# RWKV-6 attention and an MLP on one core: the first round wholly on TensorE, one layout for k and r, integer additions on GpSimd

## The chip, the cores and the metric

The kernel runs on one core of a Trainium2 chip. The metric is the device time of one execution in microseconds (us), the median over several executions. Engines are named as in the profile: PE is TensorE, DVE is VectorE, ACT is ScalarE, POOL is GpSimd, and SP issues most DMAs.

## The reference

Two blocks follow each other; the inputs are fp32 except the two MLP weights, which come as float64, and the output is fp32. The first is a recurrence over 768 steps for 4 batches of 8 heads, each with a 48 x 48 state; w is a decay of each row of the state and lies between 0.8 and 0.95.

```python
batch, n_heads, seq, head_dim = (4, 8, 768, 48)
for t in range(S):
    kt, vt, rt, wt = (k[:, :, t], v[:, :, t], r[:, :, t], w[:, :, t])
    cur = np.einsum('bhd,bhe->bhde', u[None] * kt, vt)
    y[:, :, t] = np.einsum('bhd,bhde->bhe', rt, state + cur)
    state = wt[:, :, :, None] * state + np.einsum('bhd,bhe->bhde', kt, vt)
```

The second takes y as x of shape (4, 768, 384): a layer norm without offset, a product to 1536 columns, a relu, a product back to 384, and x added.

```python
xn = (x - mu) / np.sqrt(var + 1e-06) * g_ln
ch = np.maximum(xn @ w_ch1, 0.0) @ w_ch2
return (x + ch).astype(np.float32)
```

## The kernel before

**Rounds and tiles.** The work is cut into 8 rounds (a batch and half of its 768 steps), each of 3 tiles of 128 steps. Round 0 alone is worked in two parts: tile 0, and then tiles 1 and 2 (`parts_of_round`). A round has a front (the recurrence) and a back (layer norm and MLP). The MLP of round 0 uses fp32 weights as they come; rounds 1 to 7 use weights split into halves and differences, the last four rounds for both products.

**The recurrence in chunks.** Steps are taken in chunks of 64 (`C`). Within a chunk, a matrix A holds for each pair of steps (s, t) the weight with which v of step s enters y of step t. It is built by levels: at level n, blocks of 2^n steps are joined in pairs. k of the left block is multiplied by the decay from its step to the block's end, r of the right block by the decay from the block's start to its step; the products k x r of such pairs are one batch of small PE products (`quads`, into a PSUM tile named `a`), and `keep` (a masked copy, DVE) or `keep_last` (ACT) puts them into A. `grow` then multiplies k and r by the totals of w over the block (`totals`), so that the next level can join blocks twice as long. There are 6 levels (0 to 5).

**Levels 0 and 1 and the diagonal.** Before the change these are not done by PE. `inner` multiplies on tiles in natural layout (steps on partitions, four steps of a group beside each other, `Q = 4`): it writes k and r with the first two levels' decays into padded tiles `pad_k` and `pad_r` (48 values of a head in 64 places), the 4 x 4 terms of each group of four steps into `vals`, and the total decay of four steps into `w4`. `inner_by_tile` sends `vals` through DRAM (`own_d`, four DMAs out and three back into `va`), so that it lies by partition, and `place` writes it into A with a mask. `turn` has PE transpose the padded tiles into `kr` (head dimension on partitions, two heads in rows 0 to 47 and 64 to 111), `turn_w` does it for `w4`. `quads` and `grow` then start at level 2 (`LOW`). This holds for every round; in round 0 `grow` works on k and r apart and, in its second part, on half of the heads apart (two to four instructions a level); in rounds 1 to 7 `grow_both` does k and r in one instruction, which the layout of `kr` allows there.

**The rest of the front.** `turn_k` turns k back, `states` makes the chunks' states on PE and scans them on DVE, `exchange_r` and `swap` copy r and states to the other half of the partitions, and `outputs` makes y and x.

**Weights.** The 24 pieces of w_ch1 and w_ch2 are given as float64 and taken apart by `convert`: ACT makes the upper bits (`upper`), the lower bits (`lower`) and the sign; DVE shifts the upper word by 3 (`shift`) and adds the two as integers (`join`), each on 384 columns.

**What sets the order.** Every instruction is registered by `plan.add` with a list of engines that it could run on, a cost, and what it reads and writes. The order and the choice of engine are not found when the kernel is built: `ORDER` is a list of numbers in the class `Plan`, one for each registered step in the order of issue (10000 or 20000 added names the second or third engine of its list). Each engine works its instructions in that order. While it goes through the list, `order` estimates times from the costs, and where PE would wait for more than 0.35 us it issues `idle` products of zeros into a free PSUM bank instead; their number comes from that estimate and is fixed in the built program. A GpSimd step that shares the SBUF port with DVE gets a dependency on the DVE steps before it, by the flag `port`. All instructions are issued through one helper, `InOrder.call`, so the profile gives L46 as the line of nearly all of them: they are told apart by their tiles.

Of the kernel before, what the change touches and what calls it, by code (L numbers as in the profile page):

```python
# [62 lines left out]
class Plan:  # L63
# [11 lines left out]
        4, 3, 11, 7, 9, 8, 2, 12, 14, 13, 272, 5, 271, 0, 268, 269, 15, 267, 18, 19, 20, 10021, 10016, 6, 10023,  # L75
        270, 24, 25, 26, 275, 22, 111, 274, 273, 17, 29, 276, 277, 30, 280, 282, 281, 278, 105, 10279, 38, 113,
        27, 28, 114, 39, 36, 37, 123, 106, 112, 107, 124, 286, 115, 283, 284, 285, 10, 289, 125, 31, 290, 71,
        40, 291, 126, 293, 108, 99, 32, 10297, 10033, 1, 10034, 45, 294, 288, 287, 46, 47, 49, 109, 43, 127,
        129, 484, 51, 42, 41, 100, 103, 117, 131, 132, 130, 292, 295, 118, 296, 101, 44, 50, 10035, 10298, 48,
        52, 110, 53, 54, 55, 57, 128, 56, 310, 60, 102, 304, 301, 303, 481, 58, 133, 121, 64, 61, 63, 62, 66,  # L80
        302, 147, 72, 311, 65, 77, 119, 59, 67, 68, 120, 135, 313, 312, 315, 104, 10299, 149, 78, 79, 150, 116,
        134, 73, 307, 305, 122, 486, 148, 69, 80, 74, 137, 136, 436, 75, 138, 70, 76, 306, 308, 314, 309, 183,
        141, 153, 317, 318, 319, 323, 151, 487, 485, 483, 351, 482, 488, 316, 489, 81, 139, 152, 84, 140, 185,
        82, 83, 438, 85, 86, 320, 154, 10186, 87, 321, 88, 201, 322, 324, 325, 143, 451, 89, 326, 90, 327, 91,
        328, 329, 155, 184, 144, 156, 142, 331, 332, 333, 341, 330, 334, 145, 335, 342, 343, 338, 344, 187, 491,
        336, 146, 300, 340, 10092, 95, 345, 97, 353, 93, 352, 492, 10495, 354, 10494, 337, 339, 346, 347, 357,
        350, 349, 96, 94, 358, 98, 259, 348, 203, 355, 356, 361, 493, 453, 490, 497, 496, 360, 359, 455, 364,
        257, 506, 213, 362, 260, 215, 202, 216, 363, 499, 507, 247, 258, 10500, 10502, 165, 245, 255, 159, 214,
        160, 248, 177, 10365, 10366, 368, 243, 246, 367, 369, 370, 371, 372, 374, 161, 10373, 244, 256, 249,
        250, 377, 378, 379, 380, 375, 251, 376, 501, 10162, 508, 498, 503, 20204, 10517, 178, 509, 252, 510,  # L90
        179, 189, 669, 672, 171, 505, 504, 10180, 217, 205, 181, 163, 157, 188, 383, 384, 675, 524, 521, 514,
        207, 182, 439, 158, 164, 516, 511, 673, 522, 523, 670, 674, 421, 515, 190, 512, 397, 387, 513, 385, 166,
        425, 398, 218, 671, 530, 173, 386, 191, 192, 452, 525, 677, 167, 195, 456, 208, 168, 531, 518, 381, 393,
        466, 172, 169, 170, 423, 174, 175, 193, 533, 395, 176, 426, 534, 454, 194, 526, 527, 422, 437, 676, 388,
        382, 389, 390, 394, 261, 10679, 10519, 10678, 529, 265, 266, 253, 399, 254, 196, 262, 457, 263, 403,
        400, 528, 532, 206, 396, 197, 460, 424, 680, 211, 199, 463, 681, 264, 209, 536, 537, 10683, 391, 198,
        219, 237, 238, 410, 404, 468, 220, 210, 442, 392, 440, 538, 535, 539, 200, 685, 543, 684, 212, 540, 223,
        441, 231, 225, 555, 556, 401, 233, 221, 232, 415, 411, 544, 402, 239, 682, 222, 545, 235, 416, 234, 551,
        470, 427, 546, 227, 224, 547, 557, 687, 542, 552, 686, 241, 10688, 548, 228, 240, 430, 553, 445, 550,
        226, 10428, 10520, 10443, 10446, 10689, 691, 693, 558, 429, 863, 692, 549, 461, 462, 559, 560, 433, 412,  # L100
        554, 541, 405, 694, 406, 467, 236, 229, 242, 230, 561, 565, 10690, 562, 413, 471, 431, 469, 458, 414,
        566, 567, 563, 564, 695, 472, 478, 568, 464, 10434, 696, 10569, 10570, 448, 698, 697, 407, 711, 710,
        864, 860, 865, 709, 857, 702, 10449, 10705, 10706, 571, 572, 573, 574, 575, 576, 703, 444, 475, 577,
        10580, 579, 578, 704, 408, 447, 862, 712, 459, 435, 432, 450, 465, 581, 589, 590, 582, 473, 409, 591,
        583, 592, 713, 861, 417, 585, 699, 418, 608, 474, 603, 593, 715, 623, 858, 714, 479, 859, 480, 476, 700,
        701, 586, 718, 707, 584, 866, 587, 588, 419, 716, 609, 594, 719, 604, 610, 595, 624, 596, 628, 477, 618,
        10867, 10869, 721, 625, 605, 597, 626, 629, 611, 717, 720, 722, 868, 873, 630, 612, 724, 725, 874, 723,
        619, 631, 620, 632, 627, 870, 606, 10875, 613, 633, 598, 638, 634, 614, 621, 635, 607, 879, 708, 876,
        871, 796, 743, 643, 599, 727, 615, 616, 600, 617, 636, 622, 728, 637, 741, 739, 872, 644, 10877, 601,
        645, 733, 1048, 602, 880, 726, 730, 734, 735, 646, 736, 745, 731, 738, 10878, 881, 884, 737, 886, 742,  # L110
        647, 653, 639, 746, 648, 420, 826, 1050, 781, 744, 1051, 1045, 729, 885, 732, 786, 1052, 897, 654, 890,
        747, 748, 740, 892, 640, 891, 753, 749, 887, 641, 655, 754, 888, 10755, 750, 751, 889, 882, 883, 900,
        816, 1046, 658, 649, 1049, 1047, 1055, 893, 10894, 10895, 642, 1057, 659, 1053, 898, 1056, 752, 756,
        757, 650, 906, 899, 901, 651, 663, 660, 1054, 1061, 1059, 11062, 931, 11060, 11058, 11063, 11064, 11066,
        904, 10758, 759, 761, 760, 762, 763, 764, 765, 1067, 652, 10767, 10768, 10766, 777, 778, 779, 656, 664,
        773, 661, 1069, 11065, 657, 1068, 907, 769, 770, 771, 774, 775, 1138, 903, 1087, 1141, 902, 811, 665,
        801, 1135, 1136, 780, 776, 662, 772, 905, 1072, 896, 909, 911, 910, 1074, 787, 788, 1073, 802, 666, 797,
        908, 667, 912, 913, 1143, 817, 914, 1140, 932, 791, 818, 789, 819, 803, 790, 804, 792, 820, 805, 915,
        1075, 821, 831, 1086, 1088, 1142, 1137, 1139, 916, 1085, 1004, 836, 1144, 793, 1076, 798, 794, 1070,
        795, 1071, 1077, 799, 800, 782, 822, 924, 783, 823, 926, 925, 784, 921, 824, 927, 919, 785, 922, 920,  # L120
        923, 806, 832, 1078, 984, 1497, 1089, 1090, 1091, 918, 928, 917, 11081, 1079, 825, 833, 1080, 937, 933,
        807, 812, 934, 11145, 11146, 11147, 1092, 938, 834, 929, 808, 813, 814, 809, 846, 1148, 815, 810, 11149,
# [215 lines left out]
def kernel(  # L338
# [116 lines left out]
    for i in range(FC):  # L455
        plan.hold("h", f"held{i}")
        tile_("h", f"held{i}", [P, RN])
# [1315 lines left out]
    def front(part):  # L1773
# [29 lines left out]
        for lev in range(LOW, NLEV):  # L1803
            for us in apart:
                quads(part, lev, us)
# [96 lines left out]
```

## Time and profile before

| | us |
|---|---|
| median of 3 executions | 502.27 (501.8, 502.27, 507.67) |
| the profiled execution | 506.6 |
| its span, first to last instruction | 504.9 |
| DVE busy in the first 50 us | 41.9 |
| ACT busy in the first 50 us | 35.1 |
| DVE busy from 60 to 110 us | 48.5 |

The page of the profile gives busy time for each engine, then the span in 40 slices of 12.6 us, in which each digit is a busy share in tenths, the DMA traffic, the chain of work that ended last, and the costliest groups of instructions. A group's line has the engine, the operation, the tile that it writes, what it reads, the shape, and a count; then busy time and the mean duration of one in ns; then the idle time of that engine just before, and what ended it. Products in fp32 show two passes on PE for each instruction, transposes one. Where PE has an instruction named `idle`, its time is filler. Two rows of the page that the steps below rest on are these, the grow steps of all rounds together and the chain:

```profile
PE 75%; DVE 9%; ACT 9%; issue 2%; DMA 2%; SPq 1%; DVEq 0%; ACTq 0%
L46 DVE TENSOR_TENSOR kr<-kr,tot 112x1536 f32<-112x1536 f32 (+1 forms) x52 | 59.5, 1154 | 18.2 <-PE a L46 17.5
```

Grouped by shape, these 52 are 28 whole ones of 1536 columns (1787 ns each) and 24 of round 0 with 256 columns (415 ns each).

### The profile page before, as it was taken

Reading aid. Unit: us, or ns where it says so; the run is one execution under the profiler, and the core shown is the slowest. Engines: PE = TensorE matmul, PEld = TensorE weight load, DVE = VectorE, ACT = ScalarE, POOL = GpSimd, SP = SyncE. Lnnn points to the kernel's source line nnn. Section 1 sums busy time; section 2 is a strip of 40 time slices with the busy share of each in tenths; the row PEclk is TensorE's granted clock in tenths of the full one; section 3 lists DMA queues with packets and bytes.
Section 4 is the critical chain, followed back from the end, with each engine's and each line's share of the span. In section 5 each row is a group of like instructions: output and inputs, shape, how many; then the busy total and the mean of one; then the engine's idle time right before and its main releaser. Section 6 shows DMA issues by size and latency. Waiting matters only on the chain.

```text
span 504.9 us, 17798 instructions
## 1 busy us (share of the span) xinstructions
PE 488.0 (97%) x7718; PEld 408.5 (81%) x7718; DVE 359.8 (71%) x733; ACT 261.0 (52%) x596; POOL 101.3 (20%) x106
## 2 busy tenths in 40 slices
PE   9999998999999899999999899989999999999995
PEld 5676887567877578876798676778999999999995
DVE  6997899998856882696975597888957354454434
ACT  2897977954474227525545435459732333342230
POOL 6301405440224600613430530000130000000000
PEclk9998999999999999999999799999999999999999
DMA  7787374559683374237476603251231212314301
GB/s 206 185 237 210 101 193 140 106 138 231 179 233 65 65 185 114 22 97 193 81 195 165 143 4 62 23 128 28 63 111 48 62 48 78 95 48 126 95 0 47
DMA packets 105758, 57.43 MB, mean 114 GB/s; under 512 B 61904, under 2 KB 102352, under 8 KB 105680
## 3 DMA queue, kind: packets, MB, share of 16 engines
q1 hardware_dynamic: 105408, 56.10, 43.1%
q8 instruction: 60, 0.98, 0.8%
q10 hardware_dynamic: 272, 0.20, 0.1%
q14 instruction: 18, 0.15, 0.1%
HBM read 45.86 MB, written 8.06 MB: 107 GB/s over the span
## 4 chain that ended last, share of the span: by engine, by line
PE 75%; DVE 9%; ACT 9%; issue 2%; DMA 2%; SPq 1%; DVEq 0%; ACTq 0%
PE h_ps L46 27%; PE a L46 22%; PE o L46 15%; PE o_2P L46 3%; PE kr_ps L46 2%; DVE A L46 2%; PE idle L46 2%; PE o_2D L46 2%; PE xT_ps L46 2%; DVE kr L46 1%; ACT rest L46 1%; SPq L46 1%; PE kn_ps L46 1%; ACT rx L46 1%; ACT A L46 1%
## 5 line engine op out<-in xcount | busy, mean ns | idle before, releaser
L46 PE MATMUL o<-ffn,h 128*128 128x384 f32 x288 | 103.7, 501 | 0.1
L46 PEld LDWEIGHTS o<-ffn,h 128*128 128x128 f32 x288 | 53.1, 193 | 29.9 <-issue 1.2
L46 DVE TENSOR_TENSOR kr<-kr,tot 112x1536 f32<-112x1536 f32 (+1 forms) x52 | 59.5, 1154 | 18.2 <-PE a L46 17.5
L46 ACT ACTIVATE h_ps<-h_ps 128x384 f32<-128x384 f32 x84 | 39.3, 475 | 63.2 <-PE h_ps L46 58.1
L46 DVE SCALAR_TENSOR_TENSOR hL<-h_ps,hH 128x384 fp32r<-128x384 f32 x48 | 26.5, 555 | 56.8 <-ACT hH L46 56.7
L46 PEld LDWEIGHTS a<-kr 48*56 48x56 f32 (+3 forms) x3072 | 40.9, 123 | 13.3 <-issue 6.5
L46 PE MATMUL h_ps<-xd,d 128*128 128x384 f32 x204 | 50.8, 355 | 0.4 <-DMA d<-w1d 0.4
L46 PE MATMUL a<-kr 48*56 48x32 f32 (+3 forms) x3072 | 45.8, 209 | 5.0 <-issue 3.2
L46 ACT ACTIVATE hH<-h_ps 128x384 fp32r<-128x384 f32 x48 | 23.6, 491 | 48.9 <-PE h_ps L46 48.9
L46 PE MATMUL h_ps<-xhl,wl 128*128 128x384 f32 x180 | 43.8, 351 | 0.0
L46 PE MATMUL h_ps<-xhl,wh 128*128 128x384 f32 x180 | 41.2, 337 | 0.0
L46 PEld LDWEIGHTS h_ps<-xd,d 128*128 128x128 f32 x204 | 36.5, 190 | 3.1 <-PE h_ps L46 0.7
L46 ACT COPY kr<-kr_ps 112x512 f32<-112x512 f32 x48 | 27.0, 586 | 20.3 <-PE kr_ps L46 20.1
L46 PE MATMUL idle<-nought 128*128 128x384 f32 (+1 forms) x114 | 35.7, 442 | 1.3 <-DVE eps L46 1.0
L46 ACT ACTIVATE h<-h_ps 128x384 f32<-128x384 f32 (+2 forms) x60 | 24.7, 426 | 21.5 <-PE h_ps L46 21.5
L46 PEld LDWEIGHTS h_ps<-xhl,wl 128*128 128x128 f32 x180 | 31.1, 188 | 1.7 <-ACT h_ps L46 0.3
L46 PE MATMUL a<-xkr,hH 128*128 128x384 f32 x96 | 32.4, 337 | 0.0
L46 PEld LDWEIGHTS h_ps<-xhl,wh 128*128 128x128 f32 x180 | 32.3, 188 | 0.0
L46 PEld LDWEIGHTS idle<-nought 128*128 128x128 f32 x114 | 21.2, 203 | 11.8 <-issue 2.3
L46 DVE SCALAR_TENSOR_TENSOR hD<-hH,hL 128x384 fp32r<-128x384 f32 x48 | 26.7, 565 | 0.8
L46 PE MATMUL h_ps<-xf,w 128*128 128x128 f32 (+1 forms) x144 | 26.1, 333 | 0.0
L46 PE MATMUL a<-vx,A 64*64 64x48 f32 x384 | 24.8, 222 | 1.2 <-issue 1.2
(171 smaller groups left out, 1102.8 us busy)
## 6 DMA issues: line engine op xcount, KB each, us to landing
d<-w1d SPq DMA_DIRECT2D x84, 192.0 KB, 3.0
raw<-in_moe_w_ch_dram SPq DMA_DIRECT2D x24, 384.0 KB, 4.2
nat_r<-in_r_dram SPq DMA_DIRECT2D x24, 192.0 KB, 3.7
nat_w<-in_w_dram SPq DMA_DIRECT2D x24, 192.0 KB, 3.6
v<-in_v_dram SPq DMA_DIRECT2D x24, 192.0 KB, 4.6
nat_k<-in_k_dram SPq DMA_DIRECT2D x23, 192.0 KB, 3.8
w1d<-w1diff SPq DMA_DIRECT2D x12, 192.0 KB, 2.9
out_dram<-x SPq DMA_DIRECT2D x4, 576.0 KB, 4.0
```

Of the source, the lines that this page charges most:

```text
L46: ins = self.tc.keep_in_program_order(f(*args, **kw))
```

## The change

Round 0 and the weights are touched; rounds 1 to 7 keep their computation.

1. Round 0 makes all six levels on PE. `inner`, `turn_w` and `inner_by_tile` are not called for it. `turn` takes k and r from the natural tiles, and `whole_row` does the same for w: for each step of a group, `by_head` transposes one head and the 16 columns behind it to rows 0 to 63 and multiplies the second head by the identity to rows 64 to 111. The whole w lies in a third tile of the kind of `kr`, named `low0`, which also takes the totals of level 1. `lowest` is 0 for round 0, so that `quads`, `grow`, `keep` and `totals` run for levels 0 and 1 too, with two more masks.
2. The diagonal of A in round 0 is made by `own_terms`: r is multiplied by u (`ru`), one batch of 64-column products follows, and a masked copy with the mask `diagonal` takes it into A, which is set to zero at the start. u is loaded twice, by head dimension (`u_t`).
3. `kr` lies as [2, tile, pair of heads, step] instead of [2, unit, pair and tile, step], in all rounds, so that one `grow` handles k and r for either part.
4. The 24 integer additions of `convert` (`join`) run on GpSimd. The 12 shifts of w_ch1 are done in 4 instructions of 1152 columns; what waits for the addition is kept in tiles of the home `wl` instead of `h`.
5. In round 0 some copies out of PSUM, and in all rounds the halves `upper` and `scale`, may be given to DVE by the order (`shared`, `copy_on`); costs and port flags in `plan.add` are changed in some places, which issues nothing by itself. `ORDER` is replaced as a whole (2014 steps instead of 2062).

```diff
+    def by_head(to, name, c, s, rows):
+        row = tiles[name][:, c].rearrange("p j s d -> p (j s d)")
+        PE.transpose(to[0:HP], row[rows, ds(s * D, HP)], ident[rows, rows])
+        PE.matmul(to[ds(HP, D)], tiles[name][rows, c, 1, s], ident[rows, rows], start=True, stop=True)
...
+                        if rnd == 0:
+                            by_head(to[:, n, s], f"nat_{nm}0", c, s, rows)
+                            continue
                         PE.transpose(
...
+    def lowest(part):
+        return LOW if part[0] else 0
...
+    def whole_row(part):
...
+                t = tile_("a", ps, None)[0:PD, :, 0 : Q * C].rearrange("p i (a k s) -> p i s k a", a=NA, s=Q)
+                for s in range(Q):
+                    for i in range(2):
+                        by_head(t[:, i, s], "nat_w0", c, s, ds(C * i, C))
...
+    def own_terms(part):
...
+            BY[e].tensor_tensor(out=to, in0=R, in1=u_, op=ALU.mult)
...
+                            PE.matmul(
+                                t[ds(C * (i ^ j), C), j, a, c],
+                                K[rows, c0 + c, a, ds(C * i, C)], R[rows, c, a, i],
+                                start=True, stop=True,
+                            )
...
+            DVE.copy_predicated(
+                out=to, data=ps.rearrange("s b (c t) -> s b c t", c=nc),
+                mask=diagonal[:, None, None].broadcast_to([P, 2 * NA, nc, C]),
+            )
...
-    def grow(part, lev, nm, us=both_units):
...
-    def grow_both(part, lev):
+    def grow(part, lev):
         rnd, c0, nc = part
+        n, half, mine = 1 << lev, U * W, nc * NA * P
...
+            X = X[:, n : n + 2 * (half - n)].rearrange("p (m z) -> p m z", m=2)
+            X = X[:, :, ds(c0 * NA * P, mine - n)].rearrange("p m (q n) -> p m q n", n=n)[:, :, 0::2]
...
         def join():
             bits = value_().bitcast(I32)
-            DVE.tensor_tensor(out=bits, in0=bits, in1=tiles[rest_].bitcast(I32), op=ALU.add)
+            POOL.tensor_tensor(out=bits, in0=bits, in1=rest(), op=ALU.add)
...
-        plan.add("DVE", 0.353, shift, w=[key], pri=first, port=True)
-        plan.add("DVE", 0.552, join, r=[rest_], w=[key], pri=first, port=True)
+        if not first:
+            plan.add("DVE", 0.353, shift, w=[key], pri=soon, port=True)
+            plan.add("POOL", 1.05, join, r=[rest_], w=[key], pri=soon)
+        elif i % KC == KC - 1:
+            keys = [(key[0], kc) for kc in range(KC)]
+            plan.add("DVE", 0.769, shift, w=keys, pri=soon, port=True)
+            for kc in range(KC):
+                plan.add("POOL", 1.05, late[i - KC + 1 + kc], r=[(rest_[0], kc)], w=[keys[kc]], pri=soon)
...
-        inner(part)
-        turn_w(part)
+        if rnd:
+            inner(part)
+            turn_w(part)
+        else:
+            whole_row(part)
...
-        inner_by_tile(part)
-        apart = [[uu] for uu in both_units] if rnd == 0 and nc > 1 else [both_units]
-        for lev in range(LOW, NLEV):
...
+        if rnd:
+            inner_by_tile(part)
+        else:
+            own_terms(part)
+        for lev in range(lowest(part), NLEV):
+            quads(part, lev)
+            grow(part, lev)
```

## The prediction

> **What bounds the kernel now.** I read four views. First the page's busy shares and slices: TensorE has work in 488.0 of the 504.9 us, so its stream decides, provided that it is useful work.
>
> ```profile
> PE 488.0 (97%) x7718; PEld 408.5 (81%) x7718; DVE 359.8 (71%) x733; ACT 261.0 (52%) x596; POOL 101.3 (20%) x106
> PEclk9998999999999999999999799999999999999999
> L46 PE MATMUL idle<-nought 128*128 128x384 f32 (+1 forms) x114 | 35.7, 442 | 1.3 <-DVE eps L46 1.0
> ```
>
> It is not all useful: 114 passes (57 instructions) multiply zeros. Second, the timeline of TensorE for the first 60 us shows where they stand.
>
> ```profile
> 0.98 10.69 PE L46 MATMUL idle<-nought 128*128 128x384 f32 x28 [0.98 <-DVE eps L46]
> 11.60 0.44 PE L46 MATMUL kr_ps<-ident,pad_r 64*112 64x64 f32 x8
> ...
> 12.95 2.98 PE L46 MATMUL idle<-nought 128*128 128x384 f32 x10
> ...
> 24.93 0.49 PE L46 MATMUL idle<-nought 128*128 128x128 f32 x2
> 25.35 0.64 PE L46 MATMUL a<-kr 48*60 48x32 f32 x32
> 25.93 0.45 PE L46 MATMUL kn_ps<-ident,kr 48*128 48x48 f32 x8
> ...
> 27.70 1.14 PE L46 MATMUL idle<-nought 128*128 128x384 f32 x4
> ```
>
> The reader is to see that the first turn of k and r starts at 11.60, although k and r landed by 4.54 (the first VectorE multiplication of them starts then): VectorE has to make the padded tiles first. From each filler group's start to the next work the 26 groups take 34.3 us, 32 of them before 52 us. After about 52 us TensorE streams real work. Third, the table of busy time by ten microseconds and finer has the granted clock; two stretches stand out.
>
> ```profile
> 42.00:43.00 1.00, 1.00 (x6) 0.67 (x3) 1.00 (x3) 0.83 (x4) 0.00 (x0) 0.57 1.04 359
> 283.00:285.00 2.00, 2.00 (x5) 1.13 (x4) 1.97 (x3) 0.70 (x2) 0.84 (x1) 0.50 0.35 71
> ```
>
> The clock is near 0.5 from 42 to 45.5 and from 281 to 287.5, some 10 us of half speed, worth about 5 us. Fourth, the waits: after 55 us TensorE waits little (the scaled x 1.8 us, the matrix A 1.6, x 0.7, and "issue" 4.7 over the whole span).
>
> The profiled execution took 506.6 us (span 504.9 and 1.7 around it), 4.3 above the median of 502.27; one of the two slow stretches would explain that much. My sum is a difference made on the profiled execution, carried over to the median.
>
> **Part by part: the fillers (removed).** The number of fillers is in the program. Before: 26 groups, 34.3 us. After: 30 groups, smaller: 15 of one 128-column instruction, 5 of 256, 6 of 384+128, 1 of 384+256, 3 of 384+384+128, one of which opens the program. Prices from start to next start: 128 columns 0.42 (24.93 to 25.35); 384+128 1.07 (27.70 to 28.77); 384+384+128 1.61 (29.44 to 31.05). For 256 and 384+256 I estimate 0.6 and 1.3 between those. The opening group meets the slow start (its first passes stand 0.64 apart until 4.34, then 0.32): 3.0. Sum 15x0.42 + 5x0.6 + 6x1.07 + 1.3 + 2x1.61 + 3.0 = 23.2. Saved: 11.1. Two groups of before were stretched (1.92 in the slow clock, 1.53 late), so 9.7 is the low end.
>
> **TensorE work (added).** Levels 0 and 1 of the products are new in round 0: 96 instructions, six blocks of 16. A block lasts 25.93-25.35 = 0.58: 3.5 us. The own terms are 48 instructions with 64 columns instead of 32, three blocks; TensorE's 16-instruction v blocks with 64 partitions last about 0.5, so I take 0.6 each: 1.8. The turn of a tile goes from 16 single-pass transposes (0.6 us, 18.17 to 18.80) to 16 of them and 16 true products of two passes, 48 passes. The quad blocks put 32 passes into 0.58 when four parts of the array run together, so 48 take 0.87: +0.25 for each of 3 tiles, 0.75. The w turn is 24 passes a tile, 0.45, three times, against 0.4 now: +0.95. Sum 7.0. Bounds: 5 if the small tiles pack like the v blocks, 10 if the products of half tiles do not run beside the transposes. I take 7.0, as nearly all of it is priced by rows of the same kind.
>
> **VectorE in round 0 (moved).** Gone: about 25 multiplications and sums on natural tiles (13.4 us by their rows), four placings of A (2.2), 24 halves of grow (24x0.415 = 10.0). New: twelve whole grows (0.145+0.00105 per column fits the rows 0.41 at 256 and 1.76 at 1536, so six at 0.68 and six at 1.22: 11.4), six extra masked copies (4.1 at 0.43 and 0.69 for the halves and up to 1.23 for the whole diagonal), r by u 1.9, products of w 2.3, copies out of PSUM about 4. Up to the last state scan of round 0 (before: 49.2 us) its list by these prices, less the 0.08 by which successive rows overlap, is some 33 us from 5.3, so it does not forbid an earlier end; the chain over the levels (product, copy, grow) is what the fillers stand for, and they are in the sum already.
>
> ScalarE has 17 instructions fewer, and it is half idle.
>
> **Queues (SP, GpSimd).** Fourteen small DMAs of round 0's way through DRAM go off SP's queue, with their 2.5 to 4.5 us to landing. Two loads of u with 4-byte rows come in, the second as SP's fifth. SP issues one each 0.6 us, so it goes out at about 3.5 and lands near 7.1 (g_sb and u_bc: 3.8 and 3.6 us). VectorE's second copy-out is at about 6.5, and behind it stands r by u, then everything of VectorE. That is 0.6 us. On GpSimd five masks instead of three are built at the start; a mask takes 1.6 to 2.0 us there (3.78 to 5.42, 5.48 to 7.5). Level 0's is first and in time, level 1's last, at about 12.3; VectorE's masked copy of level 1 is due near 11.6 and all of VectorE stands behind it: 0.7. I add both and 0.2 for the r tile of part 1, since fillers are laid for gaps and not for these: +1.5 (0 to 3).
>
> **Integer additions to GpSimd (moved).** 24 additions leave VectorE (0.547 and 0.550 each, 13.2 us), 24 shifts become 16 (1 us less). VectorE gets about 8 us back, because multiplications of later rounds move to it from GpSimd. GpSimd's price for an int32 addition of 384 columns is not in the trace; its float rows of that shape:
>
> ```profile
> L46 POOL TENSOR_TENSOR w1diff<-wh,wl 128x384 fp32r<-128x384 f32 x5 | 5.2, 1042 | 3.6 <-ACT wl L46 3.5
> L46 POOL TENSOR_TENSOR w2t<-ffn,xkr 128x384 f32<-128x384 f32 x2 | 2.7, 1355 | 11.6 <-ACT xkr L46 11.6
> ```
>
> So 25 to 33 us on an engine that is 20% busy, and idle from 28 to 44 us. After 55 us TensorE is the bound, and what VectorE gains there can only shorten the 4.1 us of waits named above: I take -1.0, between -4.1 and a loss (rival two).
>
> **Sum.** -11.1 + 7.0 + 1.5 - 1.0 = -3.6. On the profiled execution 503.0; beside the median 502.27, 498.7: I say 498.5.
>
> **Rivals.** *One, more is won (faster).* The new order also removes the other 3.1 us of waits after 55 us, the 1.6 us "issue" stop at 279.4, and the early half-speed stretch (1.7): -3.6-3.1-1.6-1.7 = -10, 492; if the median's executions hold the late half-speed stretch too, which follows that stop within a microsecond, 3.3 more, 489. For it: each of these is a place where the order decides, and the early stretch lies in round 0. Against: the late fillers are 7 units of 128 columns before and 8 after, so the program itself still expects such gaps.
>
> *Two, the GpSimd additions hold up VectorE (slower).* The trace shows the mechanism at one place: a placing of A (two inputs in SBUF) lasts 3.39 us beside a GpSimd multiplication from 161.63 to 164.78.
>
> ```profile
> 161.63 3.15 POOL L46 TENSOR_TENSOR nat_k<-nat_k,u_bc 128x1152 f32<-128x1152 f32 x1
> 162.21 3.39 DVE L46 TENSOR_TENSOR A<-va,mask_and 128x768 int32<-128x768 int32 x1
> ```
>
> At 0.69 for 512 columns it would be 1.0 alone; it ended 0.8 us after GpSimd did. If each addition holds a grow for its whole length (1.2), the twelve of w1 put 14 us into the opening, and half of the others 7 more where VectorE is 97% busy (60 to 110 us): -3.6+21 = +17, 520. The point: 0.15 us per addition (3.6/24) eats the gain, 0.6 (13.6/24) makes a loss over 2%. Against: from 95.67 to 105.48 GpSimd multiplications last 1.43 to 1.62, near their shortest, beside a VectorE that is over 90% busy; the additions can lie beside VectorE's reads of PSUM, of which there are now more. The Trainium skill, SBUF — State Buffer, "Who interferes with whom", speaks against this part of the change: a VectorE instruction with two SBUF inputs and a GpSimd one that reads SBUF exclude each other for a whole instruction. This trace agrees at the row above (3.39 against 1.0); by that rule alone, with nothing lying well, the time would be the 520.
>
> *Three, the opening is eaten up (no gain).* Fillers keep the clock up. Now 40 units at the start become 7, ending near 4.0, before the passes speed up at 4.34. If a stretch or two of half speed like that of 42 to 45.5 (1.7 us lost) falls into the early products, or the half-tile turns don't overlap (+3), the time is 501 to 506. The Trainium skill, TensorE: Matmul & The Clock Gate, Part 1, has the clock low by default and up only after some 3.4 us of activity in a free-running window; the trace agrees in the 0.64 and 0.32 spacing, though its clock column shows 1.00 there. Taken alone, that rule would add one such stretch, 500.
>
> **Numbers.** Forecast 0.40 (494 to 501), rival one 0.37 (485 to 492), rival three 0.12 (501 to 506), rival two 0.11 (512 and up). Within 2% is 492.2 to 512.3, about what a measurement of this kernel can tell from no change: 0.40+0.12 = 0.52; faster 0.37; slower 0.11. The range 485 to 508 takes in the bounds of the TensorE work (-2, +3) and of the queues (-1.5, +1.5) and leaves out rival two.
>
> **What would show it.** In the profile after: fillers near 23 us with the first kr_ps before 5 us (else the fillers' step is wrong); a<-kr of two new forms 48*63 and 48*62 and a<-ru together near 5.3 us; TensorE without fillers from about 46 us instead of 52; GpSimd additions at 1.0 to 1.4 with grow rows still at 0.68, 1.22 and 1.79. Grow rows stretched by a microsecond beside additions mean rival two; granted clock near 0.5 before 30 us means rival three; no gap at all between 55 and 340 us means rival one.

## The result and the profile after

The changed kernel took 553.04 us (median of 4 executions, 552.54 to 561.73) beside 502.03 for the kernel before on the same chip: a ratio of 1.0987 (1.0904 to 1.107), 10% slower, outside the range of 485 to 508. The ratio is of means and leaves out the execution of 561.73, which ran slow as a whole. Its profiled execution took 553.54, span 551.8: 46.9 us more than the span of before.

The page of the changed kernel, busy shares, slices of VectorE and of the clock, and the fillers:

```profile
span 551.8 us, 18599 instructions
PE 533.9 (97%) x8143; PEld 439.4 (80%) x8143; DVE 361.0 (65%) x707; ACT 256.0 (46%) x579; POOL 109.9 (20%) x120
DVE  3113566867888968937878669979876644634434
PEclk7555767997999999999999999999999999999999
L46 PE MATMUL idle<-nought 128*128 128x128 f32 (+2 forms) x86 | 33.1, 506 | 1.0 <-DVE eps L46 1.0
```

TensorE is 97% busy as before, so the share alone tells nothing. Taking the fillers off its busy time does: 488.0 - 35.7 = 452.3 before, 533.9 - 33.1 = 500.8 now. TensorE's own work grew by 48.5 us; fillers fell by 2.6, and time without any work grew by 1.0. The sum is the 46.9 of the spans. The slices say where: the clock is 0.5 to 0.7 in the first seven, and VectorE is 10 to 30% busy in the first four. The timeline of TensorE there (start, duration, count of passes):

```profile
4.25 3.37 PE L46 MATMUL kr_ps<-ident,nat_r 64*64 64x64 f32 x24
7.55 4.98 PE L46 MATMUL kr_ps<-ident,nat_k 64*64 64x64 f32 x24
12.46 4.98 PE L46 MATMUL a<-ident,nat_w 64*64 64x64 f32 x24
...
18.09 1.08 PE L46 MATMUL a<-kr 48*63 48x32 f32 x32
...
21.32 4.98 PE L46 MATMUL kr_ps<-ident,nat_r 64*64 64x64 f32 x24
26.22 4.98 PE L46 MATMUL kr_ps<-ident,nat_k 64*64 64x64 f32 x24
```

Nine such rows of 24 passes, one each for r, k and w of three tiles, stand in the first 55 us. The first row takes 3.30 us, the others 4.7 to 4.9 at half clock, from start to the next row's start: some 42 us together. The forecast had three times 0.87 for r with k and three times 0.45 for w: 4.0. The table by ten microseconds (TensorE, weight loads, VectorE, ScalarE, GpSimd, then the granted clock):

```profile
10.00:20.00 10.00, 10.00 (x73) 6.19 (x72) 2.08 (x4) 0.58 (x1) 2.15 (x9) 0.50 0.57 185
30.00:40.00 10.00, 10.00 (x50) 5.73 (x50) 1.66 (x3) 0.00 (x0) 0.00 (x0) 0.50 0.01 2
```

50 passes in ten microseconds, at half clock, with ScalarE and GpSimd idle and VectorE busy for 1.66 us of the second stretch. VectorE's masked copies waited 22.9 us for the products over the whole span, 16.4 of them in the first 66 us. The additions on GpSimd last what was forecast, and VectorE's rows of growing are at their forecast durations (1759 ns for 1536 columns, 1223 for 1024, 690 for 512):

```profile
L46 POOL TENSOR_TENSOR w<-w,held 128x384 int32<-128x384 int32 x12 | 13.6, 1163 | 13.2 <-PE a L46 10.1 <-ACT kr L46 3.0
L46 POOL TENSOR_TENSOR ffn<-ffn,rest 128x384 int32<-128x384 int32 x12 | 12.5, 1061 | 19.7 <-ACT rest L46 8.8 <-DVE w L46 5.1 <-DVE ffn L46 2.6
```

### The profile page after: what moved, and what is told of

It is laid out like the page before. It is cut to its first block, busy times and chain, and to the rows that moved or that the text cites. A ratio compares the mean times of both kernels' runs of the same rounds, so it can differ in the third digit from the quotient of the medians.

```text
span 551.8 us, 18599 instructions
## 1 busy us (share of the span) xinstructions
PE 533.9 (97%) x8143; PEld 439.4 (80%) x8143; DVE 361.0 (65%) x707; ACT 256.0 (46%) x579; POOL 109.9 (20%) x120
## 5 line engine op out<-in xcount | busy, mean ns | idle before, releaser
L46 DVE TENSOR_TENSOR kr<-kr,tot 112x1536 f32<-112x1536 f32 (+2 forms) x36 | 56.9, 1580 | 13.3 <-PE a L46 12.9
L46 PEld LDWEIGHTS a<-kr 48*32 48x32 f32 (+5 forms) x3264 | 48.3, 135 | 16.4 <-issue 6.5
L46 PE MATMUL a<-kr 48*32 48x32 f32 (+5 forms) x3264 | 53.0, 220 | 6.3 <-DVE A L46 3.8
L46 ACT COPY kr<-kr_ps 112x512 f32<-112x512 f32 x46 | 25.2, 587 | 56.8 <-DVE kr L46 30.1
L46 PE MATMUL h_ps<-xd,d 128*128 128x384 f32 x204 | 49.0, 347 | 0.0
L46 DVE COPY_PREDICATED A<-mask,a 128x768 f32<-128x768 int8 (+2 forms) x31 | 28.1, 907 | 23.0 <-PE a L46 22.9
L46 PE MATMUL idle<-nought 128*128 128x128 f32 (+2 forms) x86 | 33.1, 506 | 1.0 <-DVE eps L46 1.0
L46 PEld LDWEIGHTS idle<-nought 128*128 128x128 f32 x86 | 19.0, 252 | 9.2 <-issue 5.1
```

The source lines that it names most:

```text
L46: ins = self.tc.keep_in_program_order(f(*args, **kw))
```

## The experiments

Each run is compared with runs of the kernel before on the same chip; their medians were 501.2 to 504.8, so medians of two runs from different chips can lie some 3 us apart for that reason alone. The edits are shown in their main lines, and `...` marks what is left out.

**1. The order of passes within a turn.** The changed kernel alternates a transpose (first head) and a two-pass product (second head). Three edits of that and nothing else.

All transposes of r and k first, then all products:

```diff
-    def by_head(to, name, c, s, rows):
+    def first_head(to, name, c, s, rows):
...
+    def second_head(to, name, c, s, rows):
...
+            for head in (first_head, second_head) if rnd == 0 else ():
+                for n, nm in enumerate("rk"):
+                    for s in range(Q):
+                        for i in range(2):
...
+                            head(to[:, n, s], f"nat_{nm}0", c, s, ds(C * i, C))
```

> The turns of round 0 with all first heads (transposes) of a tile ahead of all second heads (products by the identity), instead of one of each in turn; nothing else changes. Theory one, a transpose and a true product of TensorE do not overlap, so each change from one to the other drains the array: 16 pairs a tile have 32 changes, now 2; a k and r turn falls from 8 to 10 us to about 1.2, a w turn from 5 to about 0.7, the clock stays up, and the whole falls by some 50 us to 497 to 504, where the forecast's own sum stood. Theory two, the small products with 48 columns are slow by themselves (8 passes of 0.2 us each per four heads): the turn stays above 5 us a tile and the whole above 535. Theory three, GpSimd's integer additions cost as much as the turns: turns fall, but the whole stays above 512.

511.02 us, ratio 1.0216 (1.0166 to 1.0265): 42 us came back with the same passes. The theory's 497 to 504 is missed by 7 us; experiments 3 and 4 follow what is left.

First heads by true products too, the alternation of heads kept:

```diff
-        PE.transpose(to[0:HP], row[rows, ds(s * D, HP)], ident[rows, rows])
+        PE.matmul(to[0:HP], row[rows, ds(s * D, HP)], ident[rows, rows], start=True, stop=True)
```

> The first heads made by true products too (64 columns, two passes instead of one), in the same alternation as in the change. Theory one (the change of kind drains the array): nothing changes kind within a turn, so a k and r turn of 64 passes takes 1.2 to 1.6 us and the whole is 498 to 507. Rival: what is slow is the alternation of the two column halves of the array in one PSUM bank, whatever the kind; then a turn stays at 6 us or more and the whole above 535.

509.69 us (one run), within 3 us of the theory's 498 to 507. More passes than in the changed kernel, less time.

Two transposes (both halves of the rows), then two products:

```diff
+                for s in range(Q):
+                    for head in (first_head, second_head):
+                        for i in range(2):
...
```

> Two first heads (both row halves), then two second heads: half as many changes of kind as in the change. Theory one: a turn takes about half as long (3.3 us at full clock, 5 at half clock, instead of 6.6 and 9.9), the whole 520 to 535. If a change of kind cost nothing, the whole would stay at 553.

518.20 us (one run). First turns on TensorE's timeline, of the grouped one, the one with products alone, and the one by two:

```profile
4.24 0.41 PE L46 MATMUL kr_ps<-ident,nat_r 64*64 64x64 f32 x8
4.62 0.41 PE L46 MATMUL kr_ps<-ident,nat_k 64*64 64x64 f32 x8
4.96 0.65 PE L46 MATMUL kr_ps<-ident,nat_r 64*48 64x64 f32 x16
5.45 0.61 PE L46 MATMUL kr_ps<-ident,nat_k 64*48 64x64 f32 x16
5.99 0.99 PE L46 MATMUL a<-ident,nat_w 64*64 64x64 f32 x24
```

```profile
4.27 0.79 PE L46 MATMUL kr_ps<-ident,nat_r 64*64 64x64 f32 x32
4.87 0.66 PE L46 MATMUL kr_ps<-ident,nat_k 64*48 64x64 f32 x32
5.31 0.68 PE L46 MATMUL a<-ident,nat_w 64*48 64x64 f32 x32
```

```profile
4.27 1.84 PE L46 MATMUL kr_ps<-ident,nat_r 64*64 64x64 f32 x24
6.04 1.76 PE L46 MATMUL kr_ps<-ident,nat_k 64*64 64x64 f32 x24
```

From row to row, r and k take 1.75, 1.04 and 3.46 us. At full clock the changed kernel's take 2 x 3.30 = 6.6. It has 31 changes from transpose to product or back within a turn of r and k, the one by two 15 and about half the time, the grouped one a single change, the one with products none. The changes cost, not the passes: beyond the grouped order, (6.6 - 1.75)/30 = 0.16 us for each. At each of them two things may change, the kind of pass and the shape of the tile of the array that it takes.

**2. Kind or shape?** Four edits of the kernel before, in the turns of all 8 rounds (24 turns of r and k, 0.59 us each), where rounds 1 to 7 have no fillers that could hide a loss. First the kind alone: the second half of the rows by a product of the same 112 columns.

```diff
-                        PE.transpose(
...
+                        row = tiles[f"pad_{nm}{rnd}"][rows, s, c].rearrange("p j d -> p (j d)")[:, 0:PD]
+                        if i == 0:
+                            PE.transpose(to[:, n, s], row, ident[rows, rows])
+                        else:
+                            PE.matmul(to[:, n, s], row, ident[rows, rows], start=True, stop=True)
```

> The kernel before with one edit: in the turn of r and k of all 8 rounds (24 tiles), the second half of the positions is turned by a true product and not by a transpose, so that the two kinds of pass stand by turns (per tile 8 transposes and 8 products of two passes). Theory 'a change of kind empties the array': a turn of 8 changes there and back takes 8 x 0.41 = 3.3 us where it takes 0.5 now, some 2.8 us more for each of 24 tiles: 560 to 575 us, less what the fillers of the opening take up, so 550 to 575. Rival 'only the pairs of the changed kernel are slow, because both write one half of a bank or read the same rows': here the two kinds use different rows of the array and different banks, the turns take 0.6 to 0.8 us, and the time is 504 to 512 us.

530.19 us (one run, before 503.48), between the 550 to 575 of the theory and the 504 to 512 of its rival: both missed. The control, all 16 by products:

```diff
-                        PE.transpose(
...
+                        PE.matmul(to[:, n, s], row, ident[rows, rows], start=True, stop=True)
```

> The control to the run in which the kernel before alternated transposes with products in its turns of all 8 rounds (24 turns, 0.59 us each before, 1.71 us alternated, +26.7 us in all): here all 16 passes of a turn are true products. Theory 'the change of kind costs, not the product': 16 products of two passes at the rate of the run with products alone (64 passes in 1.04 us) are 0.5 to 0.9 us a turn, so 503 to 511 us. Rival 'true products of 64 rows are slow whatever stands beside them': at least as slow as the alternation, which has half of them: 1.7 to 2.9 us a turn, 530 to 560 us.

532.30 us (one run, before 504.56). One turn of the first run and one of the second, each up to the work behind it:

```profile
117.30 0.70 PE L46 MATMUL kr_ps<-ident,pad_r 64*112 64x64 f32 x9
...
119.01 2.20 PE L46 MATMUL o<-ffn,h 128*128 128x384 f32 x6
```

```profile
117.88 1.00 PE L46 MATMUL kr_ps<-ident,pad_r 64*112 64x64 f32 x16
118.72 0.95 PE L46 MATMUL kr_ps<-ident,pad_k 64*112 64x64 f32 x16
119.60 2.20 PE L46 MATMUL o<-ffn,h 128*128 128x384 f32 x6
```

A turn took 1.71 us in the first and 1.72 in the second: 24 x 1.12 = 26.9 is nearly the whole difference to before. The two are equal because the 8 products of one half of the rows take 8 x 0.214 us one behind the other, and whatever the other half does lies beside them. So changing the kind at one shape costs nothing here, my theory of it fell, and the rival of the control (a product is dear in itself) was right: 0.214 us against 0.59/8 = 0.074 for a transpose.

In this run the two kinds use different rows of the array, while in the changed kernel a transpose and its product use the same ones. The kernel before has changes of kind on the same rows, where transposes of x over the whole array stand between products over the whole array:

```profile
176.04 0.49 PE L46 MATMUL xT_ps<-ident,xn 128*128 128x128 f32 x3
176.37 2.10 PE L46 MATMUL o<-ffn,h 128*128 128x384 f32 x6
178.31 0.49 PE L46 MATMUL xT_ps<-ident,xn 128*128 128x128 f32 x3
```

From start to start the three transposes take 0.33 us, 0.11 each, and the six passes 1.94, 0.32 each, the step between passes inside the group too. So a change of kind at one shape costs nothing that shows on the same rows either.

Then the shape alone, with no transposes: the first half of the rows by one product of 112 columns, the second by two, of 64 and 48 columns.

```diff
+                        for cols in (ds(0, PD),) if i == 0 else (ds(0, HP), ds(HP, D)):
+                            PE.matmul(to[cols, n, s], row[:, cols], ident[rows, rows], start=True, stop=True)
...
```

> The kernel before, its turns of r and k in all 8 rounds made of true products alone, with no transposes: the first half of the rows by one product of 112 columns, the second half by two, of 64 columns into positions 0 to 63 and of 48 into positions 64 to 111, and the two shapes stand by turns (8 times each per tile). Theory 'a change of shape empties the array' (from a tile of 64 rows and all columns to tiles of 64 rows and 64 columns and back): products of 112 columns alone took 1.72 us a turn, 0.214 each in two row tiles side by side; with 16 changes of shape nothing lies side by side and each change costs 0.1 to 0.17 us more: 4 to 6 us a turn, 585 to 630 us, and longer than the same products grouped by shape. Theory 'the change from transpose to product is what costs': there is none here, the halves lie side by side, 1.7 to 2.2 us a turn, 530 to 545 us.

665.09 us (one run, before 501.94), above the 585 to 630 of the first theory. The same products ordered by halves, so that the shape changes twice a turn:

```diff
+            for i in range(2):
+                for n, nm in enumerate("rk"):
+                    for s in range(Q):
...
```

> The same products as in the run beside it, in another order: in each turn first the 8 of the first half of the rows, then the 16 of the second, so that the shape changes twice a turn and not 16 times. Theory 'a change of shape empties the array': 8 x 0.214 = 1.7 us and then 1.0 to 1.7 us, 2.8 to 3.6 us a turn, 555 to 580 us, 30 to 60 us shorter than the run beside it. Theory 'the change from transpose to product is what costs': grouping by rows only takes away the overlap of the halves: also 2.8 to 3.4 us a turn, but here longer than the run beside it by 20 to 40 us.

564.84 us (one run). A turn at full clock of the first (r and k), and one of the second:

```profile
404.84 2.43 PE L46 MATMUL kr_ps<-ident,pad_r 64*112 64x64 f32 x24
407.20 2.43 PE L46 MATMUL kr_ps<-ident,pad_k 64*112 64x64 f32 x24
409.56 0.78 PE L46 MATMUL h_ps<-xhl,wl 128*128 128x384 f32 x2
```

```profile
129.78 0.99 PE L46 MATMUL kr_ps<-ident,pad_r 64*112 64x64 f32 x8
130.62 0.95 PE L46 MATMUL kr_ps<-ident,pad_k 64*112 64x64 f32 x8
131.49 0.68 PE L46 MATMUL kr_ps<-ident,pad_r 64*64 64x64 f32 x16
131.98 0.65 PE L46 MATMUL kr_ps<-ident,pad_k 64*48 64x64 f32 x16
132.56 2.20 PE L46 MATMUL o<-ffn,h 128*128 128x384 f32 x6
```

4.72 us against 2.78 for the same passes: (4.72 - 2.78)/14 = 0.14 us for each change of shape. In the alternating kernel the clock falls as well (a turn at 465.8 us takes 7.68), in the grouped one much less: the mean granted clock is 0.881 and 0.971. So 24 turns at 1.94 us, 47 us, are about half of the 100 us between the two runs. A change of shape alone, with no transpose near it, costs about what a change cost in the changed kernel (0.14 and 0.16 us). The Trainium skill, TensorEngine Tiling (Array Packing), Tiling Modes, "Key Properties", has it that changing the tiling mode, not merely the tile, drains TensorE; these runs agree and price it. The same page, under Restrictions, has fp32 transposes shut out from column tiling, which would give the transpose of 64 columns another shape than the product beside it; no run here shows that step by itself. That the changes of the changed kernel are changes of shape is therefore argued: kind at one shape is ruled out, and shape alone has the price.

**3. The additions on GpSimd.** Alone, in the kernel before with its old order:

```diff
-            DVE.tensor_tensor(out=bits, in0=bits, in1=tiles[rest_].bitcast(I32), op=ALU.add)
+            POOL.tensor_tensor(out=bits, in0=bits, in1=tiles[rest_].bitcast(I32), op=ALU.add)
...
-        plan.add("DVE", 0.552, join, r=[rest_], w=[key], pri=first, port=True)
+        plan.add("POOL", 1.05, join, r=[rest_], w=[key], pri=first)
```

> The kernel before with one part of the change alone: the 24 integer additions on GpSimd instead of VectorE, in the old order. Forecast's view: TensorE's stream hides them; 499 to 506. Rival two of the prediction: each addition holds a VectorE step with two SBUF inputs for 1 to 1.4 us, 512 or more.

510.41 us, ratio 1.0195 (1.0159 to 1.0231), 9.2 us for 24 additions, 0.38 each. Its groups show VectorE rows held up and more fillers:

```profile
L46 DVE TENSOR_TENSOR kr<-kr,tot 112x1536 f32<-112x1536 f32 x28 | 52.4, 1873 | 17.3 <-PE a L46 17.0
L46 DVE SCALAR_TENSOR_TENSOR w1rest<-w,g_sb,wh 128x384 f32<-128x384 f32 x12 | 11.3, 958 | 0.9 <-POOL ffn L46 0.9
L46 POOL TENSOR_TENSOR ffn<-ffn,rest 128x384 int32<-128x384 int32 x12 | 17.3, 1451 | 11.2 <-ACT rest L46 2.9 <-DVE w L46 2.5 <-DVE kr L46 2.1
L46 PE MATMUL idle<-nought 128*128 128x384 f32 (+2 forms) x128 | 41.7, 456 | 1.0 <-DVE eps L46 1.0
```

Before, the first was 1787 ns and the second 610: 2.4 and 4.1 us longer in all. The rule that the forecast weighed (the Trainium skill, SBUF — State Buffer, "Who interferes with whom") agrees in direction with both; by a whole addition of 1.2 us each, the twelve of the second row would have lost 14 us. The 0.38 is the price of the move, not of the hold-up alone: in the planner's estimate TensorE waits longer with the dearer additions, so that the program also lays 14 passes of filler more (128 for 114, 41.7 us for 35.7). How much of the 9.2 us each of the two makes is not separated.

In the new order, with the turns made of products alone, all 24 back on VectorE in their places of the order:

```diff
-            POOL.tensor_tensor(out=bits, in0=bits, in1=rest(), op=ALU.add)
+            DVE.tensor_tensor(out=bits, in0=bits, in1=rest(), op=ALU.add)
...
```

> The changed kernel with two edits: every head of round 0 is turned by a true product (as in the run before that took 509.7 us), and the 24 integer additions of the weights are back on VectorE, in the places of the order that they have on GpSimd. Theory 'the additions on GpSimd are most of what is left': added to the kernel before alone they cost 8 to 11 us, so here their return gives most of that back: 499 to 503 us, and the rows of growing (1536 columns) and placing come back to their widths of the kernel before where GpSimd no longer runs beside them. Rival 'the opening is what is left, the additions are well hidden in the new order': VectorE has only some 3 us more work per ten (24 x 0.55 us = 13 us more in all), nothing is given back: 507 to 513 us, with the clock still near half from 15 to 50 us.

514.92 us, ratio 1.02 (1.0139 to 1.0262): both expectations missed; the return did not pay. Following TensorE's work through this trace and that of the run with products alone shows where: the rows of `xT_ps` at 55.55 us are 5.1 earlier, by 144 us the kernel is 0.9 late, then 5.1 late at 301. The opening gains, and the stretch of the later additions loses. My reading was that these stand in places of VectorE's list made for GpSimd; no run separates that from the work itself, which VectorE now has more of. So only the first nine went back (those before 60 us):

```diff
-            POOL.tensor_tensor(out=bits, in0=bits, in1=rest(), op=ALU.add)
+            (DVE if i < FC - KC else POOL).tensor_tensor(out=bits, in0=bits, in1=rest(), op=ALU.add)
...
```

> The run with every head turned by a true product (509.7 us, additions on GpSimd) with one edit: the first nine of the twelve additions of the first weights, which fall into the first 60 us, are back on VectorE; the other fifteen stay on GpSimd. With all 24 back on VectorE, the same point of TensorE's work was reached 4.4 us earlier at 65 us (a granted clock of 1.0 where it was 0.5 from 35 to 55 us), and that lead was lost again between 115 and 140 us (6 us) and between 270 and 290 us (4 us), where VectorE had the late additions in places of the order that were made for GpSimd. Theory 'the nine cost the opening, the fifteen are hidden': the lead of 4 to 5 us at 65 us stays: 503 to 506 us. Rival 'the lead is lost whatever the late additions do, since the order waits at about 130 us for something else (a transfer, VectorE)': 508 to 511 us.

509.63 us, ratio 1.0127 (1.0085 to 1.0169), in the rival's range: by the two traces it is 4 us ahead of the run with products alone at 55 us and still at 110, the lead is lost in two steps near 146 and from 270 us, and 0.8 is left at the end. The two runs are from different chips; beside the kernel before on its own chip this one is 5.1 us longer and the other, a single run, 8.5, so how much of the lead stays is not settled.

**4. The clock of the opening.** From 10 to 30 and 30 to 50 us the granted clock was 0.74 and 0.63 with products alone, and TensorE stood still for 2.03 us at 13 us without a wait that the profile names. More fillers for it (in the kernel of all 24 on VectorE):

```diff
+            early = 8.0 < t < 60.0
-            if idle and e == "PE" and t - free["PE"] > 0.35:
+            if idle and e == "PE" and t - free["PE"] > (0.05 if early else 0.35):
-                n = int((t - free["PE"] - 0.1) / (idle[1] * (2 if t < 5.0 else 1)))
+                n = int((t - free["PE"] - 0.1) / (idle[1] * (2 if t < 5.0 else 1))) + (2 if early else 0)
...
```

> The kernel of e5 with more fillers: in the first 60 us each wait of TensorE that the planner sees gets two fillers more (46 blocks of 384 columns in the program where e5 has 33). Theory 'the opening loses by the half clock': TensorE's own work of 15 to 55 us runs at a granted clock of 0.5 because the array is too little used; with more fillers the clock stays near full there, and the kernel is 2 to 5 us faster than e5. Rival 'the opening is bound by VectorE, the clock costs nothing there': the clock rises, the time stays within 1 us of e5. Third: the fillers stand in the way of the work behind them, and it is 2 to 4 us slower (13 blocks of about 0.33 us are 4.3 us).

520.92 us, ratio 1.0343 (1.0272 to 1.0414): with and without them the clock was 0.83 from 10 to 30 us and 1.00 from 30 to 50, so the half clock that the first theory set out from was not there with all additions on VectorE. The third theory holds, and 6 us is more than it gave: fillers that did not raise the clock were only in the way.

Half the instructions, each over all 128 rows, beside the run of 509.63 us with the nine on VectorE (the lines taken out are those of the changed kernel):

```diff
-        PE.matmul(to[0:HP], row[rows, ds(s * D, HP)], ident[rows, rows], start=True, stop=True)
-        PE.matmul(to[ds(HP, D)], tiles[name][rows, c, 1, s], ident[rows, rows], start=True, stop=True)
+        PE.matmul(to[0:HP], row[:, ds(s * D, HP)], ident, start=True, stop=True)
+        PE.matmul(to[ds(HP, D)], tiles[name][:, c, 1, s], ident, start=True, stop=True)
...
```

> The same kernel, and each product of a turn takes all 128 rows of a tile at once (64 or 48 columns into 128 positions), so that a turn of r and k has 16 products and not 32, and TensorE has half the instructions in the turns; the evictions go by r and k and not by halves. Theory 'the count of small instructions starves TensorE': the stretch of 2 us at 13 us in which TensorE stands without anything that the profile shows to wait for, and the half clock behind it (15 to 25 us), go: 2 to 4 us faster than the run beside it. Rival 'VectorE sets the pace of the opening': the gap is filled with another wait, within 1 us of the run beside it.

504.69 us, ratio 1.0017 (0.9983 to 1.0051): as long as the kernel before. Its turn is longer (1.79 us from row to row, 1.04 in narrow tiles in the run with products alone), and yet it is 4.9 us faster than the run beside it (2.3 by the spans). Windows of that run and of this one:

```profile
10.00:30.00 20.00, 16.72 (x449) 13.20 (x448) 12.81 (x22) 9.60 (x20) 4.94 (x15) 0.74 0.64 193
30.00:50.00 20.00, 17.61 (x456) 13.21 (x457) 17.27 (x37) 14.11 (x39) 2.36 (x1) 1.00 0.69 185
```

```profile
4.25 1.09 PE L46 MATMUL kr_ps<-ident,nat_r 128*64 128x128 f32 x16
5.17 1.04 PE L46 MATMUL kr_ps<-ident,nat_k 128*48 128x128 f32 x16
```

```profile
10.00:30.00 20.00, 18.10 (x478) 14.55 (x474) 14.33 (x25) 10.99 (x25) 4.82 (x13) 1.00 0.70 213
30.00:50.00 20.00, 17.74 (x428) 12.72 (x426) 18.58 (x41) 13.78 (x37) 2.36 (x1) 1.00 0.67 185
```

The stop and the slow clock from 10 to 30 us are gone. Whether fewer instructions or full rows did it, this run can't say.

The nine additions on GpSimd again, which is the changed kernel with nothing but its turns mended:

```diff
-            (DVE if i < FC - KC else POOL).tensor_tensor(out=bits, in0=bits, in1=rest(), op=ALU.add)
+            POOL.tensor_tensor(out=bits, in0=bits, in1=rest(), op=ALU.add)
```

> The run whose products take all 128 rows of a tile at once (504.7 us, as long as the kernel before), with one edit undone: the first nine additions of the first weights are on GpSimd again, as in the changed kernel, so that it is the changed kernel with nothing but the turns of round 0 mended. Theory 'the additions on GpSimd cost the opening also where the turns are mended': with the narrower products they cost 4.3 us at 65 us of the span, of which 0.1 to 1 us was left at the end; here, with no other loss in the opening, 2 to 4 us are left: 506.5 to 509 us. Rival 'the turn was the whole loss, the additions are hidden': 504 to 506 us, within the interval of the run beside which it stands.

508.11 us, ratio 1.0097 (1.0055 to 1.0138), within the theory's range: the turns were 45 to 47 of the 51 us lost (45 between the medians, 47 beside the kernel before of each chip), and with the nine additions on GpSimd it takes 3.4 more (2.4 by the spans). The same two windows of that run:

```profile
10.00:30.00 20.00, 18.29 (x476) 14.55 (x472) 14.65 (x26) 11.67 (x27) 6.52 (x15) 1.00 0.76 221
30.00:50.00 20.00, 18.63 (x358) 14.09 (x359) 12.69 (x27) 10.67 (x27) 5.10 (x4) 0.57 0.55 150
```

Is that the slow clock, that is, too few fillers laid for them? Two units more for each group from 24 to 48 us:

```diff
+            early = 24.0 < t < 48.0
...
-                n = int((t - free["PE"] - 0.1) / (idle[1] * (2 if t < 5.0 else 1)))
+                n = int((t - free["PE"] - 0.1) / (idle[1] * (2 if t < 5.0 else 1))) + (2 if early else 0)
...
```

> The run with the turns mended and all 24 additions on GpSimd (508.1 us) with one edit: each group of fillers that the planner lays between 24 and 48 us gets two units of 128 columns more (about 0.2 us each at full speed; 8 groups, some 3 us). In that run the granted clock was 0.57 from 30 to 50 us, a product block took 1.83 us where it took 1.08 in the run with nine additions on VectorE, and TensorE was 5.3 us behind at 45 to 50 us. But VectorE's rows beside the three additions at 28.2 to 32.1 us are stretched by only 0.4 to 0.6 us each, and the fillers behind them are 3 units there and 8 in the other program. Theory 'the additions cost through the clock: the fillers laid for them are too few': with more fillers the clock stays at 1.0 from 30 to 50 us, and the time falls to 504 to 506 us. Rival 'the additions hold up VectorE itself': the clock rises, and the time stays at 507 to 510 us. Third: two units are not enough or come too late, the clock stays near 0.57 from 30 to 50 us, 507 to 511 us, and the two are not told apart.

507.60 us, ratio 1.0064 (1.003 to 1.0098). The clock from 30 to 50 us rose from 0.57 to 0.83, the time by its interval did not move: as the rival said, though some 7 us from 34 to 40 stayed at 0.50. What part of the 3.4 us goes by VectorE and what by the clock stays open.

## Why the prediction was wrong

**The step that failed** is in the work added to TensorE: "The quad blocks put 32 passes into 0.58 when four parts of the array run together, so 48 take 0.87." That row holds products of one shape. A turn of r and k in the changed kernel changes 31 times between transpose and product; at 0.14 us, the price of a change of shape, that is 4.3 of its 6.6 us, and the rest is passes with nothing beside them. At the half clock that follows it takes 9.8. The nine rows of 24 passes cost 42 us where 4.0 were laid out, +38; with the turns mended, TensorE's own work fell from 500.8 to 462.1 (491.6 - 29.5 in the run of 508.11 us). The bound of 10 for the whole term was no bound: I had "half-tile turns don't overlap (+3)", which prices missing overlap and not the changes.

**The rest of that term** held. The two new levels and the own terms were put at 5.3; in the run of 504.69 us their three rows are 1.8, 1.8 and 2.2 us.

**Fillers.** The number was right (43 instructions, 86 passes), the price not: 33.1 us busy instead of 23.2. The working took their price from rows at full clock, and many ran at half clock, but that is a part of it only: in the run of 504.69 us, whose clock was 1.00 from 10 to 50 us, the fillers still take 28.6 (94 passes there).

**Queues.** Of the 1.5, about the size of one term came true, for another mask. In the run of 508.11 us VectorE's first masked copy, that of level 0 at 8.16 us, waits 0.6 us for GpSimd's `mask`, which the working had in time; that of level 1, at 14.73, waits for nothing. The 0.6 for u does not show: r by u starts at 6.82, right behind the copy ahead of it. In the changed kernel no masked copy waits for a mask, as all of it lies behind the turns.

**Additions, -1.0.** The sign was wrong for all 24 in the old order (+9.2) and for the nine of the opening in the new one (+3.4). VectorE's rows beside additions are longer, as rival two had it, but the price of the move is 0.38 us for each in the old order and 0.3 to 0.4 for each of the nine, above its point of 0.15 and below its 0.9, and it holds more than the hold-up: fillers and clock move too. For all 24 in the new order the sign is not shown: there 24 on GpSimd took 509.69 and 24 on VectorE 514.92, on two chips and in an order made for GpSimd.

**Rivals.** Three was named for the right place (the opening, half speed before 30 us, half-tile turns) and priced at 501 to 506; its sign, a granted clock near 0.5 before 30 us, came true (0.50 from 10 to 60 us), but its mechanism lacked the changes, and the top of its price was 47 us too low. Nothing speaks for rival one.

**With the turns mended**, and the nine additions on VectorE, the sum comes out as +7.4 of work (forecast 7.0), -7.1 of fillers (-11.1) and -0.3 of waits, by the page of the 504.69 us run: 0 instead of -3.6, within 2%. That the work comes so near its 7.0 is partly luck: the nine rows of turns take some 8 us there where 4.0 were laid out, and the profiled execution of before ran at a mean granted clock of 0.988 where this one has 0.997. No version here beat the kernel before.

## What to carry to other kernels

Price small products by rows of the same sequence, not of the same size: where neighbours differ in kind and in the tile of the array that they use, count the changes, 0.14 to 0.16 us each here, and group them or give all one kind and shape, even at the cost of more passes. Look at granted clock and busy share together, for a TensorE that is 100% busy at clock 0.5 is the symptom. And moving work back in an order that was made without it has to be measured over the whole kernel: the additions' return paid in the opening and was lost behind it.

## What the runs showed of the hardware

- Changing the shape of the tile costs 0.14 us between two-pass fp32 products whose moving side has 64 columns (4.72 and 2.78 us a turn); changing between transpose and product at one shape costs nothing that shows (1.71 and 1.72 us a turn on different rows, steps of 0.11 and 0.32 us on the same).
- Rows of TensorE that are busy throughout did not keep the clock up: 10.00 of 10.00 us busy at 0.50 from 10 to 60 us of the changed kernel. The Trainium skill, TensorE: Matmul & The Clock Gate, Part 1, ties the clock to activity in a window; here the busy share of the profile is no measure of that activity.
- With a turn of 32 passes over all rows, 1.79 us, the kernel was 4.9 us faster than with one of 64 passes in narrow tiles, 1.04 us; the clock from 10 to 30 us was 1.00 where it had been 0.74. That the clock alone made the difference is not shown, as a stop of 1.75 us went too.
